# Attention scores fetched through a second DMA queue: 126 late fetches move from SyncE to ScalarE

## The chip, the cores and the metric

One core of a Trainium2 chip runs the whole program. The metric is the device time of one execution in microseconds (us); before and after are compared on the same chip.

## The reference

Eight batches of 12-head attention over 448 positions, in which the scores are mixed over the heads before the softmax and the probabilities after it, followed by a layer of three matrix products. Cut to what is computed:

```python
scores = scale * np.matmul(q, k.transpose(0, 1, 3, 2))          # 8 x 12 x 448 x 448
scores = np.einsum('bhij,hg->bgij', scores, w_pre)
attn = np.exp(scores - np.max(scores, axis=-1, keepdims=True))
attn = attn / (np.sum(attn, axis=-1, keepdims=True) + 1e-09)
attn = np.matmul(np.einsum('bhij,hg->bgij', attn, w_post), v)
x = attn.transpose(0, 2, 1, 3).reshape(B * S, H * D)            # 3584 x 768
h = (x @ w1) * (x @ w2) @ w3                                    # width 1024
return h @ w_out                                                # 3584 x 768
```

## The kernel before

The attention part is a loop of steps n (lines 891 to 986), 45 row blocks of 10 rows for each of 8 batches, 360 steps and 6 more. Two row blocks make a pair, number m = n // 2, and most work is done once for a pair:

- **qk** (line 167) computes raw scores on TensorE (psq) and copies them from PSUM with two ScalarE copies into a tile st (lines 180, 181). SyncE stores st into a tensor raw_d in device memory, ordered by row.
- **fetch(m)** (line 196) reads the score rows of pair m back from raw_d into a tile r, so that heads lie on partitions: two requests of 60 x 2 x 448 numbers (line 203), or four smaller ones where a pair crosses the end of a batch (line 210). There are two buffers r, so fetch(m) waits for mix(m-2), which reads the older one. It is issued at step n = 2m - 4, at the start of the step.
- **mix(m)** (line 215, at an odd step) multiplies r by w_pre on TensorE into two PSUM banks psm, which every mix uses. **largest(m)** (line 224) takes the row maxima on VectorE (mn), **exp(m)** (line 231) two ScalarE activations that read psm, and **scale(m)** (line 240) the reciprocals ri and scaled weights w. mix(m+1) writes the banks that exp(m) has read.
- **post(m)** (line 251) mixes the probabilities over heads (pso); two ScalarE copies put the result into mt (line 275).
- **av** (line 293) multiplies by v, and its result goes to the expert layer, for later batches through a tensor x_d.

Between these lies the expert layer as single matmuls ("atoms", lines 508 to 570 for batches 0 and 1, from line 606 for pairs of batches), handed out by advance(). It streams weights through tiles wu (line 394) and, from about step 107 to step 187, also makes sums of weights and stores them in tensors s_d (lines 451 to 506). Pair layers load x_d (line 619).

The order of instructions on each engine is the order in which the code issues them; each engine works through its list in that order. Before the change SyncE (SP) issues every DMA: fetches r, stores of st into raw_d, loads of kq, v, wu and x, stores of s_d, x_d and out. The build gives each DMA one of eight completion semaphores (DMAHW0 to DMAHW7), in turn. A DMA waits, on the engine that issues it, until the transfer that held its semaphore before has landed, besides what its own data and buffer need.

In a step with an even n the code issues, in this order: fetch(m+2), the stores and loads that are due (do_later), largest(m), atoms, exp(m), more atoms, av. In an odd one: due stores and loads, scale, atoms, post(m-1), mix(m+1), the copies of post and qk.

Of the kernel before, what the change touches and what calls it, by code (L numbers as in the profile page):

```python
# [15 lines left out]
B, H, S, D = 8, 12, 448, 64  # L16
# [10 lines left out]
HK = H * IH  # L27
PP = 64
# [5 lines left out]
LATE = 2 * NB + GB + 2  # L34
# [16 lines left out]
class Kernel:  # L51
# [144 lines left out]
    def fetch(self, m):  # L196
        r = self.rp.tile([128, 2, S], F32, tag="r", name=f"r{m}", bufs=2)
        self.rs[m] = r
        b, t = divmod(2 * m, NB)
        if t + 1 < NB and self.width(2 * m + 1) == IB:  # L200
            src = self.raw_d[b][t * IB:(t + 2) * IB].rearrange("(c s i) h j -> s (i h) c j", c=2, s=2)
            for s in range(2):
                self.nc.sync.dma_start(r[s * PP:s * PP + HK], src[s])
            return
        for c in range(2):
            b, t = divmod(2 * m + c, NB)
            for s in range(2):
                k = self.half(2 * m + c, s)
                src = self.raw_d[b][t * IB + s * IH:t * IB + s * IH + k].rearrange("i h j -> (i h) j")
                self.nc.sync.dma_start(r[s * PP:s * PP + H * k, c], src)  # L210

    def half(self, n, s):
        return min(IH, self.width(n) - s * IH)
# [840 lines left out]
```

## Time and profile before

| what | value |
|---|---|
| median of 3 runs | 1438.72 us (1436.74 to 1440.12) |
| the profiled execution | 1439.32 us, its span 1437.5 us |
| granted TensorE clock, mean | 0.989 |
| DMA queue q1, the one that SP's requests use | 413.94 MB, 87.4% of 16 engines |
| requests r<-raw_d | 344 of 210 KB and 32 smaller ones, 5.0 us to landing at line 203 |

PE is TensorE's matmuls, ACT ScalarE, DVE VectorE, POOL GpSimd, and SPq the DMA requests that SyncE issues. A row of a timeline has start, length, engine, line, operation, tiles and the number of instructions put together. A row of waits reads "engine line <- what ended the wait: us in total, times, longest". The profile shows no busy time for requests; a request's length in a timeline is the time that its queue was occupied by it, not the transfer.

### The profile page before, as it was taken

The numbers are of one execution on the slowest core, as the hardware profiler recorded it, in microseconds if no ns is written. First come the engines' busy times: TensorE is split into PE (matmuls) and PEld (weight loads), VectorE is DVE, ScalarE is ACT, GpSimd is POOL, SyncE is SP. The second block draws the span as 40 slices with busy tenths as digits, with TensorE's granted clock in tenths as the row PEclk, the third lists the DMA queues.
The fourth block names the chain that finished last, engine by engine and source line by source line (L and its number), as shares of the span: only waits on it lengthen the run. The fifth ranks groups of instructions, "written<-read, shape, count | busy, mean of one in ns | idle before, by whom it ended". The sixth has DMA issues, their size and how long they took to land.

```text
span 1437.5 us, 45779 instructions
## 1 busy us (share of the span) xinstructions
PE 1382.0 (96%) x18684; PEld 1053.5 (73%) x18684; DVE 741.6 (52%) x1497; ACT 832.5 (58%) x1952; POOL 619.8 (43%) x754
## 2 busy tenths in 40 slices
PE   5779999999999999999999999999999999999998
PEld 2357786776677667776777777777777777899988
DVE  6867567667544545432444436333445446345563
ACT  4867666777766656665656557556555445432231
POOL 2433233434433544532345336334335446446693
PEclk8989999999999999999999999999999999999999
DMA  9998789999989999999989978799879757698775
GB/s 294 368 330 274 241 271 314 318 312 312 330 281 348 350 363 318 373 357 338 289 268 295 320 259 280 249 318 350 285 223 297 239 176 224 195 337 270 230 232 172
DMA packets 203761, 416.87 MB, mean 290 GB/s; under 512 B 20528, under 2 KB 120112, under 8 KB 203472
## 3 DMA queue, kind: packets, MB, share of 16 engines
q1 hardware_dynamic: 203552, 413.94, 87.4%
q8 instruction: 149, 2.44, 0.7%
q14 instruction: 60, 0.49, 0.1%
HBM read 279.77 MB, written 134.09 MB: 288 GB/s over the span
## 4 chain that ended last, share of the span: by engine, by line
PE 80%; DMA 11%; DVE 4%; ACT 2%; issue 1%; POOL 1%; SPq 0%; DVEq 0%; POOLq 0%; ACTq 0%
PE e L703 20%; PE psa L302 11%; PE pso L261 10%; PE psm L221 8%; PE psq L175 7%; PE eg L523 5%; PE psf L361 4%; PE eo L554 4%; PE e2o L703 4%; PE e3o L703 4%; PE e1o L703 3%; DMA wu<-w_d 3%; DMA raw_d<-st 2%; DMA r<-raw_d 2%; DMA x<-x_d 1%
## 5 line engine op out<-in xcount | busy, mean ns | idle before, releaser
L248 POOL TENSOR_SCALAR w<-wpo,ri 128x60 f32<-128x60 f32 x360 | 180.4, 517 | 487.1 <-DVE ri L246 467.8
L228 DVE TENSOR_REDUCE mn<-psm 128x1 f32<-128x448 f32 x360 | 207.6, 618 | 322.5 <-PE psm L221 322.2
L275 ACT COPY mt<-pso 128x480 f32<-128x480 f32 x352 | 197.9, 621 | 184.5 <-PE pso L261 184.3
L703 PE MATMUL e<-eh,wu 128*128 128x448 f32 x1008 | 296.7, 371 | 5.3 <-DVE c L657 3.2
L236 ACT ACTIVATE e<-psm,mn 128x448 f32<-128x448 f32 x360 | 226.8, 642 | 7.9 <-DVE mn L228 7.9
L703 PEld LDWEIGHTS e<-eh,wu 128*128 128x128 f32 x1008 | 187.5, 188 | 50.9 <-issue 25.7
L221 PE MATMUL psm<-r,wsc 60*64 60x448 f32 (+1 forms) x1440 | 194.0, 552 | 21.1 <-DVE cx L125 8.3
L261 PEld LDWEIGHTS pso<-w,e 60*64 60x64 f32 x10080 | 174.7, 134 | 50.7 <-issue 42.5
L261 PE MATMUL pso<-w,e 60*64 60x60 f32 x10080 | 198.5, 224 | 0.4 <-ACT mt L275 0.3
L703 PE MATMUL e<-el,wu 128*128 128x448 f32 x504 | 186.9, 371 | 0.0
L302 PE MATMUL psa<-mt,v 128*64 128x150 f32 (+1 forms) x2304 | 156.9, 292 | 3.2 <-ACT st L180 3.2
L175 PE MATMUL psq<-kq 64*64 64x448 f32 x1176 | 156.4, 542 | 3.4 <-ACT st L180 3.4
L302 PEld LDWEIGHTS psa<-mt,v 128*64 128x64 f32 x2304 | 143.6, 137 | 19.3 <-ACT st L180 5.9
L657 DVE TENSOR_TENSOR c<-c,e 128x448 f32<-128x448 f32 x168 | 101.6, 617 | 87.5 <-PE e L703 82.9
L180 ACT COPY st<-psq 128x448 f32<-128x448 f32 x162 | 86.4, 533 | 77.1 <-ACT mt L275 33.5
L523 PE MATMUL eg<-xh,wu 128*128 128x448 f32 x384 | 119.1, 380 | 4.8 <-DMA wu<-w_d 4.8
L642 POOL TENSOR_TENSOR el<-x,eh 128x448 fp32r<-128x448 f32 x90 | 103.8, 1173 | 31.8 <-ACT eh L641 26.2
L703 PEld LDWEIGHTS e<-el,wu 128*128 128x128 f32 x504 | 94.6, 188 | 22.6 <-issue 14.1
L175 PEld LDWEIGHTS psq<-kq 64*64 64x64 f32 x1176 | 61.2, 135 | 57.7 <-issue 29.7
L523 PEld LDWEIGHTS eg<-xh,wu 128*128 128x128 f32 x384 | 71.4, 189 | 37.5 <-issue 24.0
L245 DVE TENSOR_SCALAR sa<-sm 128x2 f32<-128x2 f32 x180 | 35.5, 197 | 115.1 <-ACT e L236 114.6
L181 ACT COPY st<-psq 128x448 f32<-128x448 f32 x162 | 87.6, 541 | 0.0
(99 smaller groups left out, 2007.5 us busy)
## 6 DMA issues: line engine op xcount, KB each, us to landing
r<-raw_d SPq DMA_DIRECT2D x344, 210.0 KB, 5.0
raw_d<-st SPq DMA_DIRECT2D x138, 448.0 KB, 5.7
wu<-w_d SPq DMA_DIRECT2D x104, 384.0 KB, 6.6
wu<-s_d SPq DMA_DIRECT2D x96, 384.0 KB, 4.9
wu<-w_d SPq DMA_DIRECT2D x51, 512.0 KB, 5.7
kq<-kq SPq DMA_DIRECT2D x42, 448.0 KB, 7.4
wu<-s_d SPq DMA_DIRECT2D x36, 512.0 KB, 5.1
x<-x_d SPq DMA_DIRECT2D x72, 224.0 KB, 5.8
```

The source lines that it names most:

```text
L175: nc.tensor.matmul(ps[s][z * PP:(z + 1) * PP], t[rows, q:q + PP], t[rows, k:k + S], start=True, stop=True)
L221: nc.tensor.matmul(ps[s][c * PP:(c + 1) * PP, :S], self.wsc[k], r[k, c], start=True, stop=True)
L228: self.nc.vector.tensor_reduce(mn[:, s:s + 1], self.psm[m][s][:, :S], axis=AX.X, op=ALU.min)
L236: nc.scalar.activation(e, p[:, :S], AF.Exp, bias=mn[:, s:s + 1], scale=-1.0, accum_out=sm[:, s:s + 1])
L248: nc.gpsimd.tensor_scalar_mul(w2[:, s], self.wpo, ri[:, s:s + 1])
L261: nc.tensor.matmul(self.pso[c][z * PP:(z + 1) * PP, at:at + HK], e[k, j * PP:(j + 1) * PP], w2s[k, s], start=True, stop=True)
L275: self.nc.scalar.copy(dst.rearrange("p j g (s i) -> p j s g i", s=2), src)
L302: nc.tensor.matmul(self.psa[rows, g % 3, :W], v[:, j, rows], mt[:, j, 2 * g + s, :W], start=(j == 0), stop=(j == NJ - 1))
L523: nc.tensor.matmul(p, u[:, k % (K1 // 2), x], xs[y][:, k], start=(k == 0 and t == 0), stop=(k == K1 - 1 and t == 2))
L642: nc.gpsimd.tensor_tensor(lo, x, hi.bitcast(F32), op=ALU.subtract)
L657: nc.vector.tensor_tensor(a[out], a[to[0]], p, op=ALU.add)
L703: nc.tensor.matmul(p, w[:, k, x], ops[m, k][y], start=(k == 0 and t == 0), stop=(k == nk - 1 and t == 2))
```

## The change

The fetches of pairs with 2m >= LATE = 107 are issued by ScalarE instead of SyncE: pairs 54 to 179, 126 fetches, 264 requests, from step 104 on. The call stands at the same place of the code; the earlier fetches stay on SP. Sizes, buffers and everything else are the same.

```diff
     def fetch(self, m):
         r = self.rp.tile([128, 2, S], F32, tag="r", name=f"r{m}", bufs=2)
         self.rs[m] = r
+        dma = self.nc.scalar.dma_start if 2 * m >= LATE else self.nc.sync.dma_start
...
             for s in range(2):
-                self.nc.sync.dma_start(r[s * PP:s * PP + HK], src[s])
+                dma(r[s * PP:s * PP + HK], src[s])
             return
...
-                self.nc.sync.dma_start(r[s * PP:s * PP + H * k, c], src)
+                dma(r[s * PP:s * PP + H * k, c], src)
```

The added line moves the numbers of the lines below by one (L203 becomes L204, L236 becomes L237). No instruction of PE, DVE or POOL changes its place. On ACT the requests stand behind the copies st of the odd step and ahead of the next step's exp. Around fetch 67 (r_7013, one of the fetches with four requests) ACT's list was before, with the semaphores that each instruction waits for in brackets:

```order
627 L180 COPY st_0_0_7010<-psq_0_0_0_7004 128x448 [waits DMAHW4_49,PE_49,Activation_49]
628 L181 COPY st_0_0_7010<-psq_0_0_1_7005 128x448 [waits PE_49]
629 L236 ACTIVATE e_0_7034,sm_7033<-psm_0_6996,mn_7022 128x448 [waits DVE_49,Activation_49]
630 L236 ACTIVATE e_1_7036,sm_7033<-psm_1_6997,mn_7022 128x448 [waits DVE_49]
631 L275 COPY mt_2_6696<-pso_141 128x4x2x12x5 [waits PE_49]
```

and is now:

```order
653 L180 COPY st_0_0_7010<-psq_0_0_0_7004 128x448 [waits DMAHW4_49,PE_49,Activation_49]
654 L181 COPY st_0_0_7010<-psq_0_0_1_7005 128x448 [waits PE_49]
655 L211 DMA r_7013<-raw_d 60x448 [waits DMAHW3_49,DMAHW1_49]
656 L211 DMA r_7013<-raw_d 36x448 [waits DMAHW2_49]
657 L211 DMA r_7013<-raw_d 60x448 [waits DMAHW4_49]
658 L211 DMA r_7013<-raw_d 60x448 [waits DMAHW6_49]
659 L237 ACTIVATE e_0_7034,sm_7033<-psm_0_6996,mn_7022 128x448 [waits DVE_49,Activation_49]
660 L237 ACTIVATE e_1_7036,sm_7033<-psm_1_6997,mn_7022 128x448 [waits DVE_49]
661 L276 COPY mt_2_6696<-pso_141 128x4x2x12x5 [waits PE_49]
```

Four requests, each with waits of its own, have come between the copies and exp(65). The same place on SP was before:

```order
442 L203 DMA r_6926<-raw_d 60x2x448 [waits DMAHW1_49,PE_49]
443 L203 DMA r_6926<-raw_d 60x2x448 [waits DMAHW2_49]
444 L186 DMA raw_d<-st_5_3_6923 64x896 [waits DMAHW3_49,Activation_49]
445 L186 DMA raw_d<-st_5_3_6923 64x896 [waits DMAHW4_49]
446 L394 DMA wu_6951<-w_d 128x768 [waits DMAHW5_49]
447 L158 DMA kq_1_6953<-kq 128x896 [waits DMAHW6_49]
448 L210 DMA r_7013<-raw_d 60x448 [waits DMAHW7_49,PE_49]
449 L210 DMA r_7013<-raw_d 36x448 [waits DMAHW0_49]
450 L210 DMA r_7013<-raw_d 60x448 [waits DMAHW1_49]
451 L210 DMA r_7013<-raw_d 60x448 [waits DMAHW2_49]
452 L394 DMA wu_7018<-w_d 128x768 [waits DMAHW3_49,DVE_49]
```

and is now:

```order
418 L186 DMA raw_d<-st_5_3_6923 64x896 [waits DMAHW3_49,Activation_49]
419 L186 DMA raw_d<-st_5_3_6923 64x896 [waits DMAHW4_49]
420 L395 DMA wu_6951<-w_d 128x768 [waits DMAHW5_49,PE_49]
421 L158 DMA kq_1_6953<-kq 128x896 [waits DMAHW6_49]
422 L395 DMA wu_7018<-w_d 128x768 [waits DMAHW7_49,DVE_49,PE_49]
```

The fetches 66 and 67 are gone from SP, with their waits for PE. The load of kq holds DMAHW6, and the fourth request of fetch 67 on ACT waits for the same semaphore: for that load's landing. Across the 126 fetches such pairings are with loads of wu, kq, x and v, with stores of raw_d, x_d, s_d and out, and with earlier fetches.

## The prediction

> **What bounds the kernel now.** I read the page first, then the table of windows after step 104, then who waits for whom, and last the timelines around single fetches. The profiled execution took 1439.3 us for a span of 1437.5 us, 0.6 us over the median of the runs shown (1438.7); the sum below is made against 1439.3. From the page, line 1:
>
> ```profile
> PE 1382.0 (96%) x18684; PEld 1053.5 (73%) x18684; DVE 741.6 (52%) x1497; ACT 832.5 (58%) x1952; POOL 619.8 (43%) x754
> ```
>
> TensorE is the bound, so a change counts only where it opens or closes a gap on PE. The fetches that change run from 385 us to the end of the attention part (the L203 row further down has their first and last start). Windows of that part (columns: length, busy time of the engines, granted clock, DMA share, GB/s):
>
> ```profile
> 440.00:490.00 50.00, 49.99 (x775) 36.22 (x774) 25.94 (x52) 33.80 (x80) 23.44 (x25) 1.00 1.00 337
> 490.00:530.00 40.00, 35.80 (x514) 26.35 (x515) 17.42 (x37) 21.80 (x52) 17.04 (x20) 0.91 1.03 370
> 580.00:640.00 60.00, 59.42 (x910) 44.94 (x910) 24.30 (x55) 38.67 (x95) 25.63 (x35) 1.00 1.01 368
> 640.00:700.00 60.00, 57.35 (x870) 41.94 (x866) 16.91 (x40) 35.45 (x82) 13.60 (x22) 1.00 1.00 333
> 760.00:820.00 60.00, 60.00 (x885) 45.84 (x884) 26.32 (x59) 35.83 (x87) 28.09 (x36) 1.00 1.00 320
> 820.00:940.00 120.00, 119.73 (x1710) 91.64 (x1711) 55.93 (x119) 74.02 (x174) 57.31 (x71) 1.00 0.84 268
> 940.00:1010.00 70.00, 68.53 (x986) 52.05 (x985) 26.87 (x63) 43.32 (x104) 26.30 (x36) 1.00 1.02 339
> 1120.00:1240.00 120.00, 118.58 (x1720) 93.07 (x1722) 64.04 (x127) 62.95 (x148) 58.91 (x73) 1.00 0.70 213
> ```
>
> Two kinds of stretch stand there. In six of them, 340 us together, the DMA engines are full (share 1.00 to 1.03); in the others (two are shown) the share is 0.7 to 0.84 and transfers have room. PE is nearly full in both. What PE waits for between 387 and 1250 us:
>
> ```profile
> PE eg L523 <- DMA wu<-w_d: 4.8, 4, 1.8
> PE psm L221 <- DMA r<-raw_d: 3.4, 2, 2.0
> PE e L703 <- DMA wu<-w_d: 1.4, 1, 1.4
> ```
>
> All transfers together cost PE 9.6 us there. That is the most that a better order of DMAs can give back directly. The SyncE queue itself, in the same window, waits far longer:
>
> ```profile
> SPq L203 <- PE psm L221: 241.7, 79, 6.2
> SPq L394 <- PE e L703: 14.6, 25, 1.1
> ```
>
> A fetch needs the buffer that mix(m-2) has read, so SP stands at L203 until that matmul is over, 3.1 us in each of 79 cases, and everything queued behind it stands too.
>
> **What is removed.** 264 requests and their waits leave SP. Behind them on SP are row stores (they wait for ACT's copies st, which come later than that mix), weight loads wu (they mostly wait for their buffer) and, in the full stretches, stores of split weights. Where the engines are full an earlier request does not land earlier by as much. I credit the removal with the PE waits of 9.6 us at most, and only in the stretches that are full: 4.8 + 3.4 = 8.2 us.
>
> **What is added on ACT.** The requests now stand between the copies st of one step and exp of the next. Their length, and how long a fetch takes to land, on SP between 385 and 1235 us:
>
> ```profile
> L203 SPq DMA_DIRECT2D r<-raw_d x240: 315/369/1598, 385.3 to 1224.7; - x120
> DMA to landing us min/median/max: 2.8/4.9/7.9
> ```
>
> No request on ACT stands in this trace. The nearest row says 0.32 to 1.60 us each; I take 0.4, so 0.8 us for a fetch of two, with 0.6 and 3.2 as ends. Below nothing is excluded, as ACT gives up no instruction. What hides it is the time between the end of exp(m-2) and mix(m-1), which overwrites the bank that exp reads. A step of a roomy stretch (fetch 106), ACT's rows and PE's:
>
> ```profile
> 727.82 0.54 ACT L181 COPY st<-psq 128x448 f32<-128x448 f32 x1
> 728.24 0.65 ACT L236 ACTIVATE e<-psm,mn 128x448 f32<-128x448 f32 x1
> 728.86 0.65 ACT L236 ACTIVATE e<-psm,mn 128x448 f32<-128x448 f32 x1
> 731.99 0.54 PE L221 MATMUL psm<-r,wsc 60*64 60x448 f32 x1
> ```
>
> exp ends at 729.51 and the mix starts at 731.99: 2.5 us of cover against 0.8. The roomy stretches therefore cost nothing; with 3.2 us per fetch they would cost 0.7 each.
>
> The Trainium skill's "Perfetto Trace Analysis" ("DVE / Act Engine Instruction") has ScalarE's sequencer push a compute instruction into a wait queue and go on; by it the request would be made while the copies st still run, and the 0.8 us would be nothing. No row here shows it; the sum would then be about 5 us lower.
>
> **The new wait.** The order of the changed program shows that a request waits not only for its buffer: the kernel has eight completion semaphores, used in turn, and a request waits until the transfer that last held its own has landed. On SP that held up only DMAs. On ACT it holds up exp, all copies behind it, and with them PE. The holders are mostly SP's own loads and stores. How long these take, from the page, part 6:
>
> ```profile
> wu<-w_d SPq DMA_DIRECT2D x51, 512.0 KB, 5.7
> kq<-kq SPq DMA_DIRECT2D x42, 448.0 KB, 7.4
> x<-x_d SPq DMA_DIRECT2D x72, 224.0 KB, 5.8
> ```
>
> I worked three fetches of the full stretches. Fetch 67, whose fourth request waits for the load of kq:
>
> ```profile
> 467.46 0.65 SPq L158 DMA_DIRECT2D kq<-kq  x1
> 468.29 0.65 ACT L236 ACTIVATE e<-psm,mn 128x448 f32<-128x448 f32 x1
> 468.91 0.65 ACT L236 ACTIVATE e<-psm,mn 128x448 f32<-128x448 f32 x1
> 471.03 0.54 PE L221 MATMUL psm<-r,wsc 60*64 60x448 f32 x1
> ```
>
> kq lands at 467.46 + 7.4 = 474.9; with the request exp can start at 475.3 instead of 468.29, 7.0 us late; it ends at 469.56 + 7.0 = 476.6, and the mix due at 471.03 waits 5.5 us. Fetch 90, whose second request waits for the second of two weight loads:
>
> ```profile
> 613.52 2.23 SPq L210 DMA_DIRECT2D r<-raw_d  x4
> 615.85 0.82 SPq L394 DMA_DIRECT2D wu<-w_d  x2
> 619.72 0.65 ACT L236 ACTIVATE e<-psm,mn 128x448 f32<-128x448 f32 x1
> 620.34 0.65 ACT L236 ACTIVATE e<-psm,mn 128x448 f32<-128x448 f32 x1
> 622.25 0.54 PE L221 MATMUL psm<-r,wsc 60*64 60x448 f32 x1
> ```
>
> That load begins at about 616.3 and lands at 622.0; exp is 2.7 us late, ends at 623.7, and the mix waits 1.4 us. Fetch 143, which waits for the middle one of three loads of x:
>
> ```profile
> 986.43 2.62 SPq L619 DMA_DIRECT2D x<-x_d  x3
> 989.48 0.65 ACT L236 ACTIVATE e<-psm,mn 128x448 f32<-128x448 f32 x1
> 990.10 0.64 ACT L236 ACTIVATE e<-psm,mn 128x448 f32<-128x448 f32 x1
> 992.32 0.54 PE L221 MATMUL psm<-r,wsc 60*64 60x448 f32 x1
> ```
>
> It begins at about 987.7 and lands at 993.5; exp is 4.4 us late, and the mix waits 2.8 us. The mean is 3.2 us. If SP, freed of the fetch ahead, makes each of these loads up to 1.9 us sooner (the four requests of fetch 89 above took 2.23 us) and they land sooner by that, 3.6, 0 and 0.9 are left, 1.5 on the mean. I take 3.2, because at a share of 1.0 it is the bytes ahead that decide the landing.
>
> **How often.** While PE stands, the DMA queues drain, so one stop takes the lateness off the next few fetches. I count one stop for each 50 us of full stretch: 340/50, about 7. In the roomy stretches I count none: at a share of 0.70 to 0.84 no queue builds up. That is an argument from the share, not from a row.
>
> **The clock.** After the 2 gaps near 520 us the trace shows a stretch at a lower granted clock (the third number from the right):
>
> ```profile
> 520.00:525.00 5.00, 3.03 (x10) 2.29 (x11) 2.25 (x6) 1.95 (x6) 2.73 (x3) 0.73 1.02 346
> 525.00:530.00 5.00, 5.00 (x75) 2.81 (x75) 0.98 (x3) 1.12 (x2) 0.00 (x0) 0.58 1.04 370
> ```
>
> 5 x 0.27 + 5 x 0.42 = 3.5 us of matmul time lost. New stops of 3 to 5 us should do that too; I count one more than now: 3.5 us.
>
> **Sum.** 7 x 3.2 = 22.4, less the 8.2 us of waits that PE, already stopped, no longer meets, plus 3.5: +17.7 us. 1439.3 + 17.7 = 1457.0. With 1.5 us per stop and no clock: 10.5 - 8.2, 1441.6. With 10 stops and two stretches of low clock: 32 - 8.2 + 7, 1470. That is the likeliest case's own range.
>
> **Rivals.**
> - *The freed SP queue wins* (faster). Weight loads and stores go out up to 3 us sooner, the queue never builds up, and the holders have landed when ACT asks. It decides if holders land within the cover, 2 us or less behind the copies st. Then PE loses its 8.2 to 9.6 us of waits, and with the gap at 520 the 3.5 us of clock: 1426 to 1431; half of it, 1433, is more likely. For: 241.7 us of SP's standing. Against: the full stretches move 320 to 370 GB/s, and sooner requests add no bandwidth. Chance 0.18.
> - *Nothing moves.* The requests hide in the 2.5 us of cover, the loads land as before: 1437 to 1441. The Trainium skill, "DMA: Bandwidth & Descriptors" ("Issuing engines are not separate DMA queues"), says just that: the queues share the same 16 engines, and a second issuing engine saves only issue time. Against: fetch 67's 7 us are a wait that the rule does not speak of. Chance 0.12.
> - *Stops at every full step.* The queue does not drain, since SP's next requests wait for semaphores that ACT's late fetches hold. The L203 row has 120 fetches in 839 us, one per 7 us, so 49 in 340 us; if half of them stop, that is 24 x 1.5 to 24 x 3.2, 36 to 77, less 8.2: 1467 to 1508. For: each of the three fetches worked above stops PE. Chance 0.17.
> - The forecast keeps 0.53.
>
> **Numbers.** A measurement of this kernel can tell about 0.2%, 2.9 us. Faster takes the first rival and a little of the second, 0.19; same 0.10; slower 0.71. The range 1433 to 1492 takes in half of the first rival, the second, the forecast and the lower half of the third.
>
> **What would show it.** In the changed trace ACT's exp and copies wait for DMA landings, of kq, wu, x and s_d above all, and PE's psm L221 waits for ACT e in full stretches, 15 us or more in total, with next to nothing between 820 and 940 us. ACT's requests should take 0.3 to 0.5 us. I am wrong if PE's gaps after 387 us stay under 10 us, or if they lie in the roomy stretches.

## The result, and the profile after

The changed kernel takes 1456.69 us (median of 5 runs, 1454.63 to 1459.78), the kernel before 1440.12 (5 runs, 1436.74 to 1441.91). The ratio is 1.0127, with a 95% interval of 1.0106 to 1.0148: 16.6 us slower. The profiled execution took 1454.63 us for a span of 1452.8 us, so the two profiled executions stand 15.3 us apart; all sums below are made against that. From the page of the changed kernel, line 1 (busy time, share of the span, instructions):

```profile
PE 1391.5 (96%) x18684; PEld 1057.7 (73%) x18684; DVE 744.9 (51%) x1497; ACT 840.4 (58%) x1952; POOL 621.9 (43%) x754
```

PE runs the same 18684 matmuls, yet is busy 9.5 us longer: a part of the loss doesn't show as idle time. What PE waits for between 387 and 1270 us (total, times, longest):

```profile
PE psm L222 <- ACT e L237: 4.9, 5, 2.6
PE e L704 <- ACT eh L642: 4.0, 2, 2.2
PE psm L222 <- DMA r<-raw_d: 2.6, 2, 1.4
PE psm L222 <- DMA out<-eos: 2.0, 1, 2.0
PE e L704 <- POOL el L643: 1.5, 2, 0.7
```

The waits for weights (`eg <- DMA wu`, 4.8 us before) are gone, and waits for ACT are there instead. Two kinds: the mix (psm) waits for exp, as forecast, and the experts' matmuls (e) wait for the operand splits `eh` of ACT and `el` of POOL, which the forecast did not speak of. The rows `<- DMA r` and `<- DMA out` need care. A mix waits for its row tile, for its weights and for the bank; a PE row names the one that came last by the profile. The weight loads of the same mixes, in the same window, name exp, which holds the bank:

```profile
PEld psm L222 <- ACT e L237: 15.3, 20, 2.7
PEld e L704 <- ACT eh L642: 5.5, 3, 2.6
```

Before, the first of these rows was 0.3 us, once. Now weight loads stand for exp 20 times, in 12 mixes. ACT itself, same window, the largest rows of transfers that it stood for:

```profile
ACT eh L642 <- DMA x<-x_d: 7.4, 2, 4.3
ACT e L237 <- DMA r<-raw_d: 6.5, 5, 1.7
ACT eh L642 <- DMA r<-raw_d: 4.5, 2, 2.6
ACT s L485 <- DMA raw_d<-st: 4.4, 1, 4.4
ACT eh L642 <- DMA wu<-w_d: 3.6, 1, 3.6
ACT e L237 <- DMA kq<-kq: 3.3, 1, 3.3
```

All rows of this kind together are 52.6 us in 24 places. Most of these instructions don't read the tile named: an exp reads no kq, a cast `s` no raw_d. At each of the places shown below a request on ACT ends just ahead of the instruction: it waited for the transfer which last held its completion semaphore, and the instruction stood behind it. And SyncE's queue, freed of 241.7 us of waits for the mix:

```profile
SPq L189 <- ACT st L181: 151.4, 55, 5.4
SPq L395 <- PE e L704: 90.3, 63, 3.4
```

It now stands at the row stores (L189, 17.0 us before) and at the weight loads (L395, 14.6 before). That these two rows add up to the old 241.7 is chance. All of SyncE's waits between 387 and 1270 us are 620 us now and were 479 before: it stands longer, at other instructions.

Where does the time come from? The start of each mix in the two traces, after less before, is the lag; a mix is found by its first psm row. Some of them (us):

| mix | start before | lag |
|---|---|---|
| 54 | 394.42 | 1.5 |
| 66 | 471.03 | 4.5 |
| 73 | 517.14 | 7.5 |
| 75 | 533.94 | 3.7 |
| 96 | 665.93 | 9.9 |
| 98 | 681.53 | 7.6 |
| 111 | 775.34 | 11.7 |
| 118 | 825.18 | 12.5 |
| 139 | 973.60 | 12.5 |
| 142 | 992.32 | 13.7 |
| 157 | 1095.23 | 17.8 |
| end | | 15.3 |

The 1.5 us at mix 54 are older than the first changed fetch (385 us); most of that comes from a stretch of low clock near 303 us that the changed kernel's execution has and the other has not, so the change's own share of this execution is 13.8 us. From there the lag goes up in 18 steps of over 0.3 us, 25.5 us in all, and down in ten, 11.7 us in all. The lag is read at the first matmul of a mix, so what a mix loses inside itself counts only at the next one: in the kernel before it is 0.98 us long, and at seven stops it is 1.59, since its second bank waits for the second exp. The 18 steps are thus 12 stops and six steps that trail one. From mix 118 to 139, 825 to 973 us, it stays where it is.

### The profile page after: what moved, and what is told of

Read it like the earlier page. It is cut to its first block, busy times and chain, and to the rows that moved or that the text cites. A ratio compares the mean times of both kernels' runs of the same rounds, so it can differ in the third digit from the quotient of the medians.

```text
span 1452.8 us, 45818 instructions
## 1 busy us (share of the span) xinstructions
PE 1391.5 (96%) x18684; PEld 1057.7 (73%) x18684; DVE 744.9 (51%) x1497; ACT 840.4 (58%) x1952; POOL 621.9 (43%) x754
## 5 line engine op out<-in xcount | busy, mean ns | idle before, releaser
L237 ACT ACTIVATE e<-psm,mn 128x448 f32<-128x448 f32 x360 | 225.3, 634 | 36.5 <-DVE mn L229 10.6
L222 PE MATMUL psm<-r,wsc 60*64 60x448 f32 (+1 forms) x1440 | 199.3, 557 | 25.9 <-ACT e L237 12.2
L175 PE MATMUL psq<-kq 64*64 64x448 f32 x1176 | 160.8, 545 | 3.3 <-ACT st L180 3.3
```

The costliest lines, as they stand in the source:

```text
L175: nc.tensor.matmul(ps[s][z * PP:(z + 1) * PP], t[rows, q:q + PP], t[rows, k:k + S], start=True, stop=True)
L222: nc.tensor.matmul(ps[s][c * PP:(c + 1) * PP, :S], self.wsc[k], r[k, c], start=True, stop=True)
L237: nc.scalar.activation(e, p[:, :S], AF.Exp, bias=mn[:, s:s + 1], scale=-1.0, accum_out=sm[:, s:s + 1])
```

## One stop, instruction by instruction

Fetch 67, the first that the prediction worked, in the changed kernel's timeline (start, length, engine, line; in brackets the idle time before it and what ended it), with SyncE's, ACT's and PE's rows:

```profile
468.38 0.53 SPq L158 DMA_DIRECT2D kq<-kq  x1
...
470.51 0.53 ACT L180 COPY st<-psq 128x448 f32<-128x448 f32 x1 [0.43 <-ACT mt L276]
470.61 0.34 ACTq L211 DMA_DIRECT2D r<-raw_d  x1
470.94 0.54 ACT L181 COPY st<-psq 128x448 f32<-128x448 f32 x1
470.99 3.69 ACTq L211 DMA_DIRECT2D r<-raw_d  x3
474.78 0.63 ACT L237 ACTIVATE e<-psm,mn 128x448 f32<-128x448 f32 x1 [3.30 <-DMA kq<-kq]
475.40 0.62 ACT L237 ACTIVATE e<-psm,mn 128x448 f32<-128x448 f32 x1
475.56 0.19 PEld L222 LDWEIGHTS psm<-r,wsc 60*64 60x64 f32 x2 [1.37 <-ACT e L237]
475.56 1.22 PE L222 MATMUL psm<-r,wsc 60*64 60x448 f32 x5 [1.24 <-DMA r<-raw_d]
476.17 0.14 PEld L222 LDWEIGHTS psm<-r,wsc 60*64 60x64 f32 x3 [0.43 <-ACT e L237]
```

The three requests behind the first one take 3.69 us, exp stands 3.30 us for the landing of kq, and the mix starts right after the first exp; its second bank waits for the second. The prediction put this exp at 475.3; it came at 474.78. But ACT's copies were already 3.1 us later than before (they end at 471.48, before at 468.41), so the stop added 1.5 us to the lag at the start of the mix and 2.1 at its end, not 5.5.

The route that was missed, at fetch 112 of the same kernel:

```profile
778.34 3.89 ACTq L211 DMA_DIRECT2D r<-raw_d  x3
...
782.27 0.57 ACT L642 CAST eh<-t 128x448 fp32r<-128x448 f32 x1 [3.56 <-DMA wu<-w_d]
...
782.89 0.47 PE L704 MATMUL e<-eh,wu 128*128 128x448 f32 x1 [2.18 <-ACT eh L642]
782.91 1.13 POOL L643 TENSOR_TENSOR el<-t,eh 128x448 fp32r<-128x448 f32 x1 [4.19 <-ACT eh L642]
...
784.10 0.68 PE L704 MATMUL e<-el,wu 128*128 128x448 f32 x1 [0.74 <-POOL el L643]
```

Here no exp is next on ACT but a split of the experts' operand. It has no cover: PE reads `eh` 0.05 us after it ends, and then stands again for POOL's half. At mix 111 the lag grows by 4.6 us, the largest step of all, and at mixes 156 and 157, where PE stands 1.85 us for `eh` and 0.74 for `el` near 1103 us, by 4.7 together. Both hold 1.7 us of a stretch of low clock that follows (below).

## The experiments

Each is timed against the kernel before on the same chip; the ratio to that is given with its 95% interval. The small diffs are against the kernel before; the one that puts the fetch behind exp on ACT, and those in which the helper `dma` of the change stands, are against the changed kernel.

**Is it the issuing on ACT?** All fetches stay on SyncE, and ACT gets three small copies at the place of each late fetch instead of its requests.

```diff
+        self.idle = cp.tile([128, HK], F32, name="idle")
...
                 self.fetch(m + LF // 2)
+                if n + LF >= LATE:
+                    for _ in range(3):
+                        nc.scalar.copy(self.idle, self.wpo)
```

> The fetches stay on SP as before; in the place where ACT now has the requests of a late fetch stand three short copies (128x60, into a tile that nothing reads), about 0.6 us of ACT a fetch. Landing theory (ACT stands until an earlier transfer has landed, and exp behind it is late): 1438 to 1443 us, since 0.6 us lies in the cover of 1 to 2.5 us. Issue theory (the time that ACT spends on 126 fetches is the cost): 1450 to 1458, about what the change cost. Traffic theory (a second queue makes other transfers land later): 1440, as nothing about transfers changes.

Measured: 1440.62 us against 1437.54, 1.0017 [1.0002, 1.0032]. ACT is busy 906.7 us, 74 more than before, 0.59 us for each of 126 fetches. That work costs 2.4 us, at most 4.6. So ACT's time is not it: the cover that the prediction named is there.

**Is it the wait of a request?** All fetches stay on SyncE; ACT issues one transfer of 1 KB at the place of each late fetch.

```diff
+        self.idle = cp.tile([16, 16], F32, name="idle")
...
                 self.fetch(m + LF // 2)
+                if n + LF >= LATE:
+                    nc.scalar.dma_start(self.idle, self.wpost[:16, :16])
```

> The fetches stay on SP as before; at each late fetch ACT also issues one request of 1 KB into a tile that nothing reads. It takes its turn among the eight completion semaphores, so ACT waits for the landing of an earlier transfer as with the change, while the score rows keep their queue. Landing theory: most of the loss is back, 1448 to 1475 us, with ACT e waiting for DMA landings. Issue theory: half of the loss at most (one request for two), 1444 to 1449. Traffic theory: 1438 to 1443, since 1 KB is no traffic.

Measured: 1468.2 us, 1.0207 [1.0177, 1.0238]: 126 KB of traffic that nobody reads cost 1.6 times what the change costs. One of its stops, rows of ACT and PE:

```profile
1015.21 0.54 ACT L181 COPY st<-psq 128x448 f32<-128x448 f32 x1
1020.99 0.32 ACTq L931 DMA_DIRECT2D idle<-wpost  x1
1021.35 0.56 ACT L641 CAST eh<-x 128x448 fp32r<-128x448 f32 x1 [5.59 <-DMA wu<-w_d]
...
1022.59 2.38 PE L221 MATMUL psm<-r,wsc 60*64 60x448 f32 x8 [3.43 <-ACT e L236]
```

The request is made 5.2 us after the copies end, for 0.32 us of issue; a cast, and the exp after it, stand behind it, and the mix stands 3.43 us for that exp. The profile puts the cast's wait down to a load of weights; the transfer that last held the request's semaphore in the trace is a load of x, issued at 1016.00. PE, in this kernel, between 387 and 1280 us:

```profile
PE psm L221 <- ACT e L236: 11.0, 6, 3.4
```

Neither bytes nor the fetch's new path are needed for the loss; the wait in ACT's queue is enough. This experiment has two flaws. Each of these transfers also waits for the one before it, since they write the same tile; the profile puts 1.8 us down to that, in one place. And each takes one of the eight turns, so that SyncE's own requests wait for other holders than before; what that costs was not separated. Why the experiment costs more than the change was not tried by itself. Two things differ that can make the holder of the semaphore land later against the copies: SyncE still stands 261 us at the fetches, so its loads go out as late as before, and the small request comes behind all of the step's fetch in the turn of eight, so that its holder is a later transfer: in the traces it was issued 7.0 us ahead of the request on the median, and 9.2 us for the requests of the changed kernel.

**Is it the place in ACT's queue?** The late fetches go out on ACT, as in the changed kernel, but behind exp.

```diff
-            if not odd and LF <= n + LF < N:
+            late = not odd and n + LF >= LATE
+            if not odd and LF <= n + LF < N and not late:
                 self.fetch(m + LF // 2)
...
                 self.exp(m)
+            if late and n + LF < N:
+                self.fetch(m + LF // 2)
```

> The late fetches are issued by ACT as in the change, but behind exp of the same step in place of ahead of the due stores. Landing theory: exp is no longer late, so most of the loss goes: 1438 to 1447 us; what is left is fetches that land late for their mix (PE psm waits for DMA r, 2 to 8 us) and copies mt that stand behind the request. Issue theory: ACT still spends the time, 1450 to 1457. Traffic theory: still the second queue, 1452 to 1458.

Measured: 1442.3 us, 1.0033 [1.0008, 1.0058]. Three quarters of the loss are gone. Fetch 67 in this kernel:

```profile
470.92 0.65 ACT L237 ACTIVATE e<-psm,mn 128x448 f32<-128x448 f32 x1
...
471.64 0.56 ACTq L211 DMA_DIRECT2D r<-raw_d  x1
...
473.66 0.54 PE L222 MATMUL psm<-r,wsc 60*64 60x448 f32 x1
474.22 0.32 ACTq L211 DMA_DIRECT2D r<-raw_d  x1
```

The last request still goes out only at 474.22, but exp has been issued ahead of it, and the mix starts at 473.66 with no wait. The same request on the same engine, again behind the load of kq, costs little once exp is ahead of it. Across the kernel the holders are mostly of the same kind as in the change: 188 of the 264 requests have the same semaphore and the same kind of holder. What is left is 4.2 us of PE waits for r, since some fetches go out late themselves.

**Does taking the fetch out of the head of SyncE's step help by itself?** All stays on SyncE; the late fetch goes behind the step's stores and loads.

```diff
-            if not odd and LF <= n + LF < N:
+            late = not odd and n + LF >= LATE
+            if not odd and LF <= n + LF < N and not late:
                 self.fetch(m + LF // 2)
...
                 self.load_kq(*x)
+            if late and n + LF < N:
+                self.fetch(m + LF // 2)
```

> All fetches stay on SP, but the late ones stand behind the stores and loads that are due in their step instead of ahead of them, so that SP no longer stops those while it waits for the mix. This measures the other half of the change alone, the freed SP queue. Landing theory: a small gain or none, 1434 to 1441 us, as full DMA engines do not land more bytes. Rival (the freed SP queue is worth all waits of PE for transfers, 9.6 us and a stretch of low clock): 1426 to 1432.

Measured: 1456.15 us, 1.0136 [1.0117, 1.0155]. Both theories missed this one. PE's wait and one stop of this kernel, the waits first:

```profile
PE psm L221 <- DMA r<-raw_d: 11.4, 9, 3.4
```

```profile
513.20 1.12 SPq L186 DMA_DIRECT2D raw_d<-st  x2
515.05 1.30 SPq L203 DMA_DIRECT2D r<-raw_d  x2
```

```profile
521.80 2.37 PE L221 MATMUL psm<-r,wsc 60*64 60x448 f32 x8 [3.19 <-DMA r<-raw_d]
```

Fetch 73, which the kernel before requests at 508.02, goes out at 515.05, behind the stores, and its mix stands 3.2 us for it. The head of SyncE's step is what keeps r on time; the 241.7 us that SyncE stands there are not a loss to be won back. It also says that the size of a change's loss doesn't tell its cause: this one and the change cost the same, by quite different waits.

**Where in the program?** The change only at the fetches 54 to 114, 140 to 144 and 156 to 158 (69 of 126), which hold the full stretches, and only at the other 57. The first of the two:

```diff
-        dma = self.nc.scalar.dma_start if 2 * m >= LATE else self.nc.sync.dma_start
+        dma = self.nc.scalar.dma_start if 2 * m >= LATE and not any(a <= m <= b for a, b in ((115, 139), (145, 155), (159, 179))) else self.nc.sync.dma_start
```

> ACT issues only the late fetches of the stretches with full DMA engines (pairs 54 to 114, 140 to 144, 156 to 158: 69 of 126 fetches); the others stay on SP. Landing theory: nearly the whole loss, 1451 to 1457 us. Issue theory: 69/126 of the loss, 1447 to 1450. Traffic theory: between the two, 1448 to 1455.

> The opposite: ACT issues only the fetches of the stretches with room (pairs 115 to 139, 145 to 155, 159 to 179: 57 of 126). Landing theory: holders have landed when ACT asks, 1437 to 1442 us. Issue theory: 57/126 of the loss, 1446 to 1449. A small gain from the freed SP queue may stand against either: 1 to 2 us.

Measured: full alone 1458.01 us, 1.0128 [1.0099, 1.0158]; the rest alone 1438.13, 0.9986 [0.9968, 1.0005]. The whole loss comes from the first set, and the second costs nothing that can be measured.

**Is it a second queue as such?** The late fetches on GpSimd's queue, at the same place.

```diff
-        dma = self.nc.scalar.dma_start if 2 * m >= LATE else self.nc.sync.dma_start
+        dma = self.nc.gpsimd.dma_start if 2 * m >= LATE else self.nc.sync.dma_start
```

> The late fetches go to GpSimd's queue instead of ScalarE's, at the same place of the code. ACT has no wait for a landing any more; SP is as free as in the change. Landing theory: the loss of the change goes, except what POOL's own work (scaled weights w for post, parts el) loses by standing at the requests: 1436 to 1455 us, with ACT e waiting for no DMA. Traffic theory: as the change, 1452 to 1460, since the score rows are again on a second queue.

Measured: 1442.81 us, 1.0023 [1.0006, 1.0039]. GpSimd's requests (shortest, median and longest in ns, first and last start):

```profile
L204 POOL DMA_DIRECT2D r<-raw_d x240: 637/668/900, 385.2 to 1227.0; - x120
```

The transfers are the same, SyncE is freed in the same way, ACT has no request, and exp waits for no transfer. In this run's trace GpSimd's requests take turns at eight semaphores of their own, so they do not wait for SyncE's transfers either: the run separates the traffic from the waits, but not the engine from the semaphores. Each takes 0.668 us instead of 0.323 on ACT; the loss is a fifth of the change's. A theory by which the freed SyncE or the order of the traffic makes the loss falls with this.

**A version made of the pieces**: fetches 54 to 98 on ACT behind exp, the roomy ones on ACT at the change's place, the others on SyncE.

> What the runs so far point to: fetches 54 to 98 on ACT behind exp, the fetches of the stretches with room on ACT at the place of the change, the rest (99 to 114, 140 to 144, 156 to 158) on SP as before. Landing theory: no exp is late, the waits of PE for wu and r around fetches 70, 74 and 97 go, 1433 to 1439 us beside 1438 to 1440 before. Rival (ACT's requests cost wherever they stand): 1443 to 1450.

Measured: 1439.81 us against 1440.08, 1.0003 [0.9986, 1.0020]. None of the versions beats the kernel before by an amount that can be measured.

## Why the prediction was right in the sum, and where its terms were not

The forecast was 1457.0 us; the median is 1456.69 and the profiled execution 1454.63. The main mechanism, request on ACT waits for a landing, exp and PE stand behind it, in full stretches alone, is shown by four runs: the small transfer (the wait is enough), the copies (the issue is not), behind exp (the place decides) and the split by stretches. The terms are another matter, and that the sum came within 0.3 us of the median is in part luck. The sum had 22.4 - 8.2 + 3.5 = +17.7 us; the two profiled executions differ by 25.5 - 11.7 = 13.8 us, and by 1.5 us that are older than the change. Too little was put down for stops and too little for waits that go, and the two nearly cancel.

- **The stops, 7 x 3.2 = 22.4 us.** The total is near: the steps up are 25.5 us, with 3.4 of low clock in them. Size and count are both off, in opposite directions. There are 12 stops, of 2.1 us on the mean with what trails them. The three worked fetches were put at 5.5, 1.4 and 2.8 us. Read at the end of their mixes, the first added 2.1 us. At the second (fetch 90) ACT stands 1.30 us, exp starts at 628.34 and its mix follows at 629.44 without a gap; the 0.6 us by which the lag grows there are left over from the mix before, and its own mix ends 0.3 us later. The third, fetch 143:

```profile
1003.83 0.86 ACTq L204 DMA_DIRECT2D r<-raw_d  x2
1004.74 0.57 ACT L642 CAST eh<-x 128x448 fp32r<-128x448 f32 x1 [3.07 <-DMA x<-x_d]
...
1005.98 1.22 PE L222 MATMUL psm<-r,wsc 60*64 60x448 f32 x5 [0.90 <-ACT e L237]
```

  ACT stands 3.07 us, the mix 0.90, and the lag grows by 1.1 at the start of the mix and 1.7 at its end. The step that failed: each landing was worked from the trace of before, and the mix was left at its old time. A schedule that already runs 3 us late has 3 us more of cover at the next landing where the landing does not move with it, as at fetch 67: the load of kq went out 0.9 us later than before, and ACT's copies 3.1. The landings came otherwise than the medians, too: the last request of fetch 67 goes out 6.0 us after the load of kq that it waits for (7.4 taken), that of fetch 90 10.3 us after its load of weights (5.7 taken). The large steps are elsewhere, at fetch 74 and in the splits. Fetch 74:

```profile
521.61 1.73 ACTq L204 DMA_DIRECT2D r<-raw_d  x2
...
523.43 0.51 ACT L485 CAST s<-y 128x384 fp32r<-128x384 f32 x1 [4.41 <-DMA raw_d<-st]
...
524.62 1.64 PE L222 MATMUL psm<-r,wsc 60*64 60x448 f32 x5 [2.58 <-ACT e L237]
```

- **The route by exp alone.** It misses the splits, 4.6 and 4.7 us at two places with the low clock that follows, more than a third of the steps up. The working looked at what follows the request in ACT's order at the three fetches chosen, and not at all fetches.
- **The credit of 8.2 us.** The steps down are 11.7 us, and 10.0 of them lie at mixes 70, 74 and 75, 97, 143 and 158, just where PE waited for transfers before. Three of those six waits, from the timeline of PE in the kernel before:

```profile
491.51 0.47 PE L523 MATMUL eg<-xh,wu 128*128 128x448 f32 x1 [1.52 <-DMA wu<-w_d]
...
673.91 1.25 PE L221 MATMUL psm<-r,wsc 60*64 60x448 f32 x5 [1.96 <-DMA r<-raw_d]
...
1101.28 0.44 PE L703 MATMUL e<-eh,wu 128*128 128x448 f32 x1 [1.43 <-DMA wu<-w_d]
```

  The lag falls by 1.5, 2.0 and 1.7 us there. At 74 and 75 it falls by 3.8, for two waits of 2.7 together and a part of the low clock behind them. All of the 9.6 us of waits are gone, so the credit was 1.4 us short: it left out the wait at 1101 us. The rest of the 11.7 is clock and small steps. The cause given for it in the part on what is removed is wrong, too: it is no gain of the freed queue. With the small transfers, where SyncE is not freed, the lag falls by 2.0 at mix 70 and by 2.5 at 74. Whoever is late no longer meets these waits; the clause in the sum ("that PE, already stopped, no longer meets") was the right reading.
- **The clock, 3.5 us.** The stretches of the changed kernel where the granted clock (third number from the right) is low:

```profile
520.00:525.00 5.00, 2.42 (x63) 1.75 (x62) 0.20 (x1) 1.56 (x5) 0.98 (x1) 0.98 1.06 371
525.00:530.00 5.00, 5.00 (x24) 2.34 (x23) 2.81 (x6) 2.73 (x8) 1.00 (x3) 0.68 1.04 358
...
780.00:785.00 5.00, 2.08 (x8) 1.28 (x6) 0.49 (x3) 1.80 (x5) 1.42 (x2) 0.92 0.99 351
785.00:790.00 5.00, 5.00 (x79) 3.18 (x78) 1.77 (x3) 2.02 (x4) 1.65 (x3) 0.74 0.81 271
...
1105.00:1110.00 5.00, 5.00 (x73) 3.43 (x66) 1.68 (x3) 1.66 (x4) 1.70 (x3) 0.66 1.00 324
```

  5 x (0.02 + 0.32) + 5 x (0.08 + 0.26) + 5 x 0.34 = 5.1 us, less the 3.5 that the kernel before loses at 520 us: 1.6. Two stretches were added, not one, and the old one became shorter. In the traces the granted clock is either full or half: between 387 and 1270 us it is half once for 6.8 us in the kernel before, and three times for 3.4 us in the changed one.
- **The issue on ACT.** The requests in the changed kernel (shortest, median and longest in ns, first and last start):

```profile
L204 ACTq DMA_DIRECT2D r<-raw_d x240: 321/323/1609, 387.8 to 1240.0; - x120
```

  The median lies within the forecast of 0.3 to 0.5 us, and the cost is hidden where the request need not wait. The Trainium skill's "Perfetto Trace Analysis" ("DVE / Act Engine Instruction") has the sequencer push compute into a wait queue and go on; the trace agrees: the request of 470.61 is made while the copy of 470.51 runs for 0.53 us. The same rows show where that ends, since a request that must wait holds whatever stands behind it: the one of 474.36 still comes ahead of the exp of 474.78. So the prediction's "about 5 us lower" does not follow: its sum holds one request of 0.4 us in each of 7 stops, 2.8 us, and that request has to be made behind the landing by either account.
- **The roomy stretches.** No step between 825 and 973 us, and 0.9986 with their requests alone. The argument from the share holds there. But the list of full stretches was too short: of the windows that the prediction does not show, 530 to 580 us has a share of 0.97 and 1080 to 1120 us one of 0.87, not 0.70 to 0.84. The steps at mixes 60 and 61 (435 us, 1.6 together) and at 156 and 157 (1103 us) lie outside of the six stretches. In the kernel before, the share is 0.97 from 420 to 440 us and 1.00 from 1100 to 1105.
- **The test with 15 us of psm waiting for exp.** The PE row has 4.9, which by the letter is a miss. The weight-load row has 15.3, and psm's own busy time went from 194.0 to 199.3 us: a mix whose second bank waits for the second exp is shown as a longer mix. The other sign, PE's gaps after 387 us under 10 us, could not tell: they are 18.0 us now and were 11.9 before the change.
- **The rivals.** The freed queue wins: it falls, SyncE stands 620 us in all its waits instead of 479, at other instructions, and the program is slower. Stops at every full step: it falls, 12 stops, and not 24 of 1.5 to 3.2 us. Nothing moves: it falls. The Trainium skill's "DMA: Bandwidth & Descriptors" ("Issuing engines are not separate DMA queues") says that a second issuing engine only saves issue time; as to the transfers the GpSimd run bears it out within 0.4%. As to the engine that issues, the runs with requests on ACT show a cost of which the rule does not speak, from nothing (the 57 fetches) to 2.07%.

What stays open: how the 25.5 us divide among exp, splits and clock was read from the lag and not taken apart by runs, and fetches behind exp with the splits moved ahead too were not tried.

## What to carry to other kernels

A transfer issued from a compute engine's queue is a wait for that engine, whatever its size: before moving it, list for each request what it waits for (the buffer, the semaphore of an older transfer) and the next instruction behind it that another engine needs. Put it behind that instruction, or where transfers have room. A queue that stands long at one place is not thereby a loss: see what the standing puts in order before taking it away.

## What the hardware showed that was not expected

A request of 1 KB on ACT costs as much as its wait, not as its size: 126 of them made the kernel some 30 us longer. One request takes 0.323 us on ACT, 0.369 on SyncE and 0.668 on GpSimd as the median of the rows shown. Gaps of PE of 1.85 to 2.58 us, ahead of 524, 783 and 1103 us, are each followed by a window of 5 us at a mean granted clock of 0.66 to 0.74; two gaps of 1.96 us, ahead of 673.91 in the kernel before and of 675.87 in the changed one, are not. The length of a gap alone does not decide it in these traces.
